# One kernel, its load list regrouped: four more token tiles turned by DMA, and five loads given out by ScalarE

## The chip, the cores and the metric

The kernel runs on one core of one Trainium2 chip. The metric is the device time of one execution in microseconds (us), the median over the runs. Everything below on times comes from three runs of the kernel before and from one more execution that was profiled.

The engines are called PE (TensorE, matrix products), ACT (ScalarE), DVE (VectorE), POOL (GpSimd) and SP (SyncE, which here does nothing but give out DMAs). "PEld" is the loading of PE's stationary operand, which overlaps its products.

## The reference

The output is `x + A(xn) + B(xn)`, with `xn = layernorm(x)` over 512 features of 2048 tokens, all in bf16. A is an attention over a sliding window, B a gated block that mixes tokens:

```
def A(xn):                                  # 32 heads of 16
    q, k, v = split(xn @ wqkv)
    logits[s, w] = q[s] . k[s - 2*w] / 4    # w = 0..7, masked where s - 2*w < 0
    return (softmax(logits) @ v[s - 2*w]) @ wo

def B(xn):                                  # w_in 512 x 1376, w_sp 2048 x 2048
    z = gelu(xn @ w_in)
    z1, z2 = z[:, :688], layernorm(z[:, 688:])
    return (z1 * (w_sp @ z2 + b_sp)) @ w_out
```

## The kernel before, in words

The 2048 tokens are 16 tiles of 128. Every engine has a list of named steps, written out by hand at the end of the kernel (`pe`, `act`, `dve`, `pool`, `sp`), and does them in that order; `needs` says which steps of other engines each step waits for. The names:

- `x0` to `x12`: loads of tokens (x0 to x5 one tile each, x6 two, x8 and x12 four each).
- `b`, `ag`, `gr`, `n` with a tile's number: the statistics of a tile (DVE, line 169), their aggregate (DVE, 172), the root (POOL, 175 and 176) and the normalised tile (DVE, 179).
- PE needs the normalised tile turned (features on partitions, in `xnT`). There are two ways. For tiles below `NPE`, `T` are four transposes of 128x128 on PE into a bank `aux` (line 212), and `Tc` is ACT's copy from there (line 215). For the others, `t` is one DMA transpose of the whole tile, given out by SP (line 195).
- `z` and `y`: the two halves of `xn @ w_in` (line 230), eight products of 128x344 each; `h` and `yg` are ACT's gelu of them (lines 248 and 312). They, and the products of q, k, v, go through a ring of three PSUM buffers `mm`: a product waits until ACT has emptied the buffer of the third one before it.
- `k`, `q`, `v` (line 323): eight products each, over all tokens, so that they wait for all 16 turned tiles; `kc`, `qc`, `vc` are ACT's copies. `kh0`: two small DMAs on SP that complete the first quarter of k (lines 341 and 342); `kh1` to `kh3` are the same on POOL.
- `m`, `f`, `p` (lines 357, 362, 369): the logits, products on DVE and sums by DMAs of POOL. Then softmax (X, u, C) and `a`, the weighted sum of v (lines 421, 425, 434), all on DVE. `a0.11` and `a1.11` are its last steps for either half of the tokens.
- `W0` to `W7` (line 448): `w_sp`, eight pieces of 1 MB, brought in by DMA transposes of SP into three buffers. W2 waits for `HW` on DVE (line 445), which stands behind the last logits; W3 and on wait for the mix that used their buffer.
- `M0` to `M15` (line 464): the mix `w_sp @ z2`, 32 products of 128x344 each; Mj uses piece W(j/2). `G` is ACT's copy (478), `g` the gate on DVE (480), `U` turns the gated tile by one or two DMA transposes of SP (470, 472, 473).
- `LO0` to `LO3` (line 485) load `wo` and `LO4` (488, 490; three DMAs) `w_out`; `R0`, `R1` (497) load x again. `gf`, `re`, `ao` (508, 513, 520) are the last products; `E`, `F`, `S` bring the sums out.
- `wz0`, `wz1`: weights of z2; `wy`: weights of z1; `wk`, `wq`, `wv`.

SP gives out in this order: `x0 x1 wz0 x2 wz1 x3 x4 x5 x6 x8 wy x12 wk wq wv`, then `t8` to `t15`, `W0 kh0 W1 vh W2 W3 LO0 LO1 U0 W4 U1 LO2 LO3 U2 W5 U3 U4 LO4 U5 W6 U6 U7 W7` and so on. PE does `z0 .. z7 y0 z8 y1 z9 .. z14`, then k and q (with z15 between), v, `y2 .. y15`, M0 to M15 and the last products.

One thing comes not from the lists but from how the program is built: DMAs of SP and ACT get one of eight completion counters in turn, and a DMA waits until the one before it on its counter has landed. With all of them on SP that is the DMA eight places ahead.

Of the kernel before, what the change touches and what calls it, by code (L numbers as in the profile page):

```python
# [26 lines left out]
FH = 688  # L27
# [15 lines left out]
def kernel(  # L43
# [47 lines left out]
    w_q, w_k, w_v = [wts[:, n * C * D:(n + 1) * C * D].rearrange("p (k f) -> p k f", k=C) for n in range(3)]  # L91
    w_z = [wts[:, C * (3 * D + n * FH):C * (3 * D + (n + 1) * FH)].rearrange("p (k f) -> p k f", k=C) for n in (1, 0)]
# [14 lines left out]
    z2 = z2_r[:].rearrange("p (i f) -> p i f", i=NT)  # L107
# [4 lines left out]
    xs = z1_r[:, 0:NT * D].rearrange("p (i d) -> p i d", i=NT)  # L112
# [30 lines left out]
    wq_d = A_wqkv.rearrange("(k p) f -> p k f", p=P)  # L143
    wi_d = B_w_in.rearrange("(k p) f -> p k f", p=P)
# [4 lines left out]
    def op_(name, after, f):  # L149
        assert name not in do, name  # L150
        do[name], needs[name] = f, list(after)

    def tok(i):
        return f"Tc{i}" if i < NPE else f"t{i}"

    NPE = 8
    ALLX = [tok(i) for i in range(NT)]
    ALLN = [f"n{i}" for i in range(NT)]


    def load_x(i, n):
        SP.dma_start(xs[:, i:i + n, :], x2[i * P:(i + n) * P, :].rearrange("(i p) d -> p i d", p=P))  # L162
# [15 lines left out]
    def norm(eng, i):  # L178
        eng.tensor_scalar(xn[i % 8], xs[:, i, :], mv[:, i, 0:1], rstd[:, i:i + 1], ALU.subtract, ALU.mult)  # L179
# [5 lines left out]
    for i in range(NT):  # L185
# [6 lines left out]
        else:  # L192
            op_(f"n{i}", [f"gr{i}"] + ([tok(i - 8)] if i >= 8 else []), lambda i=i: norm(V, i))
        if i >= NPE:
            op_(f"t{i}", [f"n{i}"], lambda i=i: SP.dma_start_transpose(xnT[:, :, i * P:(i + 1) * P], xn[i % 8]))
# [41 lines left out]
    for hh in range(2):  # L237
        op_(f"wz{hh}", [], lambda hh=hh: SP.dma_start(
            w_z[1][:, :, hh * FHALF:(hh + 1) * FHALF], wi_d[:, :, FH + hh * FHALF:FH + (hh + 1) * FHALF]))
    op_("wk", [], lambda: SP.dma_start(w_k, wq_d[:, :, D:2 * D]))  # L240
    op_("wq", [], lambda: SP.dma_start(w_q, wq_d[:, :, 0:D]))
    op_("wv", [], lambda: SP.dma_start(w_v, wq_d[:, :, 2 * D:3 * D]))
    op_("wy", [], lambda: SP.dma_start(w_z[0], wi_d[:, :, 0:FH]))
    op_("b16", [], lambda: G.dma_start(b16[:], B_b_sp.rearrange("(j p) -> j p", p=P)))

    def z2_gelu(i, t):
# [125 lines left out]
    for c, th in BUF:  # L372
        n = f"{c}{th}"
# [131 lines left out]
    def gated_full(i, start, stop, c=slice(0, D)):  # L505
        th, t0 = i // 8, (i % 8) * P
        for m in range(MF):
            PE.matmul(po[i][:, c], uT[th][:, m, t0:t0 + P], wout[:, m, c], start=(start and m == 0), stop=(stop and m == MF - 1))  # L508

    def gated_rest(tiles, start, stop):  # L510
        for i in tiles:
            r, t0 = 64 * (i // 2 % 2), (i % 8) * P
            PE.matmul(po[i], uT[i // 8][r:r + FREST, MF, t0:t0 + P], wout[r:r + FREST, MF, :],  # L513
                      start=start, stop=stop, tile_position=(r, 0))
# [6 lines left out]
                          start=(start and d == 0), stop=(stop and d == DH - 1), tile_position=(32 * g, 0))  # L521

    U = [[f"U{j}" for j in range(8 * th, 8 * th + 8)] for th in range(2)]
    EVM = [f"G{j}" for j in range(NT)] + ["Bc", "Tc4"]
    for n in (0, 1):
        op_(f"gf{n}", LO + U[0] + EVM, lambda n=n: [gated_full(i, True, False) for i in groups[n]])
        op_(f"re{n}", [f"gf{n}"], lambda n=n: gated_rest(groups[n], False, False))
# [27 lines left out]
    for n, c in enumerate(halves):  # L555
        i = groups[3][3]
# [1 line left out]
        op_(f"Sl{n}", [f"Fl{n}"], lambda n=n, c=c: (SP, A)[n].dma_start(out2[i * P:(i + 1) * P, c], o_of(i)[:, c]))  # L558
# [39 lines left out]
    dve += """zt0 zt1 zt2 zt3 zt4 zt5 zn0 zn1 zn2 zn3 zt6 zt7 zn4 zn5 zn6 zn7
# [62 lines left out]
```

## Time and profile before

| | |
|---|---|
| three runs | 205.86, 209.40 and 208.57 us; median 208.57 |
| profiled execution | 206.27 us, of which 204.5 are the span from the first to the last instruction |
| granted clock of PE in the profiled execution | 0.999 |
| PE, PEld, DVE, ACT, POOL busy | 95%, 59%, 86%, 44%, 21% of the span |
| moved by DMA | 33.63 MB, mean 164 GB/s |

The profile has a page of summaries and views that can be asked for one stretch: the timeline (start, duration, engine, line, operation, and in brackets the idle time ahead of it with what ended it), the chain of waits (the work that ended last, followed back), and tables of busy time by stretch. In all of them times are from the start of the span. SPq is SP giving out a DMA: its duration is the giving out alone, and the landing comes later. PE's clock is full throughout, so a difference in PE's work is one of work and of waits.

### The profile page before, as it was taken

How to read it: one execution, taken by the hardware profiler on the slowest of the kernel's cores; microseconds unless marked ns; L12 is line 12 of the kernel's file. 1: busy time of each engine (PE TensorE's matmuls, PEld its weight loads, DVE VectorE, ACT ScalarE, POOL GpSimd, SP SyncE). 2: the span in 40 equal slices, each digit the busy share in tenths (PEclk: the TensorE clock that was granted, in tenths of full speed). 3: DMA queues.
4: the chain of work that ended last, by engine and by line, in shares of the span. 5: the costliest groups of instructions: out<-in, count | busy, mean ns of one | idle time of the engine just before them, and what ended most of it. 6: DMA issues, size and time to landing. Idle time of an engine off the chain costs nothing.

```text
span 204.5 us, 4534 instructions
## 1 busy us (share of the span) xinstructions
PE 194.8 (95%) x1935; PEld 121.1 (59%) x1935; DVE 175.3 (86%) x202; ACT 89.9 (44%) x130; POOL 43.2 (21%) x72
## 2 busy tenths in 40 slices
PE   7899999999999999999999999999696999999991
PEld 2476666666666666666666666666464654444441
DVE  5899894897899999959999999999996699995314
ACT  2497797795569996654453311111111110052000
POOL 5577122059995033110000000000000000000000
PEclk9999999999999999999999999999999999999999
DMA  5999474919999999992699997979789499006023
GB/s 164 355 379 178 103 151 89 205 13 185 196 184 182 200 192 152 172 185 44 133 207 253 141 220 163 251 78 247 179 86 226 111 262 275 0 3 202 23 86 103
DMA packets 68388, 33.63 MB, mean 164 GB/s; under 512 B 56064, under 2 KB 66192, under 8 KB 68240
## 3 DMA queue, kind: packets, MB, share of 16 engines
q1 hardware_dynamic: 65696, 24.79, 56.3%
q0 software_dynamic: 2528, 8.48, 22.8%
q8 instruction: 15, 0.25, 0.5%
q10 hardware_dynamic: 144, 0.07, 0.1%
q14 instruction: 5, 0.04, 0.1%
HBM read 10.03 MB, written 2.10 MB: 59 GB/s over the span
## 4 chain that ended last, share of the span: by engine, by line
PE 81%; DMA 11%; DVE 5%; SPq 1%; issue 0%; DVEq 0%
PE mm L464 31%; PE mm L323 20%; PE mm L230 13%; DMA wsp<-in_B_w_sp_dram 7%; PE mm L520 7%; PE mm L508 6%; DVE stats L169 2%; DMA xnT<-z 2%; DMA z<-in_A_x_dram 2%; PE aux L508 2%; PE mm L513 1%; DVE z L179 1%; SPq L162 1%; DVE z L552 1%; DVE mv L172 1%
## 5 line engine op out<-in xcount | busy, mean ns | idle before, releaser
L464 PE MATMUL mm<-z,wsp 128*128 128x344 bf16 x512 | 75.2, 309 | 3.3 <-DMA wsp<-in_B_w_sp_dram 3.3
L464 PEld LDWEIGHTS <-wsp 128*128 128x128 bf16 x512 | 49.9, 98 | 28.4 <-DMA wsp<-in_B_w_sp_dram 4.0
L323 PE MATMUL mm<-xnT,wts 128*32 128x512 bf16 x768 | 41.9, 380 | 0.0
L230 PE MATMUL mm<-wts,xnT 128*128 128x344 bf16 x256 | 39.2, 309 | 0.6 <-ACT xnT L215 0.5
L323 PEld LDWEIGHTS <-wts 128*32 128x32 bf16 x768 | 28.4, 139 | 13.2 <-issue 0.6
L421 DVE TENSOR_TENSOR prod<-vp,a_sb 128x4096 bf16<-128x4096 bf16 x16 | 36.1, 2284 | 0.0
L478 ACT ACTIVATE qk<-mm,b_col 128x688 bf16<-128x688 f32 x16 | 13.3, 832 | 50.0 <-PE mm L464 47.8
L230 PEld LDWEIGHTS <-xnT 128*128 128x128 bf16 x256 | 24.3, 98 | 13.3 <-ACT xnT L215 0.9
L357 DVE TENSOR_TENSOR prod<-qk 128x4096 bf16<-128x4096 bf16 x12 | 26.9, 2288 | 2.1 <-DMA qk<-qk 1.9
L425 DVE TENSOR_TENSOR prod<-prod,prod 128x8192 bf16<-128x8192 bf16 x6 | 26.5, 4418 | 0.0
L336 ACT CAST qk<-mm 128x1024 bf16<-128x1024 f32 x16 | 16.2, 1012 | 7.8 <-PE mm L323 7.8
L312 ACT ACTIVATE z<-mm 128x688 bf16<-128x688 f32 x16 | 11.8, 748 | 5.6 <-PE mm L230 5.2
L520 PE MATMUL mm<-wts,xnT 32*128 32x512 bf16 x192 | 14.2, 374 | 0.0
L508 PE MATMUL mm<-wts,qk 128*128 128x512 bf16 x60 | 13.8, 379 | 0.0
L508 PEld LDWEIGHTS <-qk 128*128 128x128 bf16 x85 | 8.2, 98 | 9.4 <-issue 0.8
L362 POOL DMA_DIRECT2D prod<-prod x12 | 10.7, 1178 | 12.5 <-DVE prod L357 12.5
L248 ACT ACTIVATE z<-mm 128x688 bf16<-128x688 f32 x16 | 11.9, 745 | 2.2 <-PE mm L230 2.1
L169 DVE BATCH_NORM_STATS2 stats<-z 128x6 f32<-128x512 bf16 x16 | 10.7, 672 | 1.9 <-DMA z<-in_A_x_dram 1.9
L552 DVE TENSOR_TENSOR z<-mm,wsp 128x512 bf16<-128x512 f32 x6 | 3.9, 684 | 9.9 <-PE mm L520 5.6
L520 PEld LDWEIGHTS <-xnT 32*128 32x128 bf16 x256 | 6.4, 93 | 7.6 <-issue 0.8
L480 DVE TENSOR_TENSOR z<-qk,z 128x688 bf16<-128x688 bf16 x16 | 8.0, 510 | 3.3 <-ACT qk L478 3.3
L546 ACT CAST z<-mm 128x512 bf16<-128x512 f32 x6 | 3.2, 598 | 13.7 <-PE mm L520 12.3
(81 smaller groups left out, 170.7 us busy)
## 6 DMA issues: line engine op xcount, KB each, us to landing
prod<-prod POOLq DMA_DIRECT2D x12, 512.0 KB, 8.7
wts<-in_A_wo_dram SPq DMA_DIRECT2D x4, 512.0 KB, 6.6
wsp<-in_A_x_dram SPq DMA_DIRECT2D x2, 1024.0 KB, 5.8
out_dram<-z SPq DMA_DIRECT2D x15, 128.0 KB, 1.8
wts<-in_A_wqkv_dram SPq DMA_DIRECT2D x3, 512.0 KB, 9.3
z<-in_A_x_dram SPq DMA_DIRECT2D x2, 512.0 KB, 7.3
wsp<-z POOLq DMA_DIRECT2D x2, 512.0 KB, 8.3
wsp<-wts POOLq DMA_DIRECT2D x2, 512.0 KB, 8.3
```

The lines of the kernel that those rows point to most:

```text
L169: V.bn_stats(stats[:, i, :], xs[:, i, :])
L230: PE.matmul(t[:, hh, 0:FHALF], xnT[:, kc, i * P:(i + 1) * P], w_z[part][:, kc, hh * FHALF:(hh + 1) * FHALF], start=(kc == 0), stop=(kc == ...
L248: A.activation(z2[:, i, :].rearrange("p (a b) -> p a b", a=2), t[:, :, 0:FHALF], ACT.Gelu_apprx_tanh, **total)
L323: PE.matmul(t[32 * g:32 * g + 32, dd, :], w, r, start=(kc == 0), stop=(kc == C - 1), tile_position=(0, 32 * g))
L336: op_(f"{a}c{p}", [f"{a}{p}"], lambda: A.copy(home(a, p), t[:].rearrange("p d (t s) -> p d t s", t=2)))
L357: V.tensor_tensor(pr, q, k, ALU.mult)
L421: return lambda: V.tensor_tensor(dst, vp[:, :, th, off:off + GS], a_sb[:, th, W - 1 - w].unsqueeze(1).broadcast_to([P, DH, GS]), ALU.mult)
L425: return lambda: V.tensor_tensor(dst, dst, x, ALU.add)
L464: PE.matmul(t[:, hh, 0:FHALF], w[:, k, (j % 2) * P:(j % 2 + 1) * P], z2[:, k, hh * FHALF:(hh + 1) * FHALF], start=(k == 0), stop=(k == NT ...
L478: lambda: A.activation(gs[j % 3].rearrange("p (a b) -> p a b", a=2), t[:, :, 0:FHALF], ACT.Identity, bias=b_col[:, j:j + 1]))
L508: PE.matmul(po[i][:, c], uT[th][:, m, t0:t0 + P], wout[:, m, c], start=(start and m == 0), stop=(stop and m == MF - 1))
L520: PE.matmul(po[groups[n][g]], op[32 * g:32 * g + 32, th, d, s * P:(s + 1) * P], wo_r[32 * g:32 * g + 32, d, :], start=(start and d == 0), ...
```

## The change

Five things are edited together:

- `NPE` goes from 8 to 4: tiles 4 to 7 are turned by DMAs of SP (`t4` to `t7`) instead of by PE and ACT.
- `x12`, `wy`, `wk`, `wq`, `wv` are given out by ACT, at places inside its list, instead of by SP.
- SP's list: `x2` stands ahead of `wz0`; `t4` follows `x8` directly; `LO2 LO3` go from between U1 and U2 to behind W5, `LO4` from ahead of U5 to behind W6.
- PE's list: `B` (one small transpose of b_sp) and `y0` stand earlier, and `y2` stands between z11 and z12 instead of behind v7. ACT's list follows this.
- DVE's list: `n2` stands ahead of `b3`.

```diff
-    NPE = 8
+    NPE = 4
...
-        SP.dma_start(xs[:, i:i + n, :], ...)
+        (A if i == 12 else SP).dma_start(xs[:, i:i + n, :], ...)
...
-    op_("wk", [], lambda: SP.dma_start(w_k, wq_d[:, :, D:2 * D]))
+    op_("wk", [], lambda: A.dma_start(w_k, wq_d[:, :, D:2 * D]))
...
-    EVM = [f"G{j}" for j in range(NT)] + ["Bc", "Tc4"]
+    EVM = [f"G{j}" for j in range(NT)] + ["Bc", "Tc3"]
...
-    pe = """wu T0a T0 z0a z0A T1 z0B T2 z1 T3 z2 T4 z3 T5 z4 T6 z5 T7 B z6 z7 y0 z8 y1 z9 z10 z11 z12 z13 z14
+    pe = """wu T0a T0 z0a z0A T1 z0B T2 z1 T3 z2 B z3 z4 z5 z6 y0 z7 z8 y1 z9 z10 z11 y2 z12 z13 z14
...
-        v0 v1 v2 v3 v4 v5 v6 v7 y2 y3 y4 y5 y6 y7 y8 y9 y10 y11 y12 y13 y14 y15
+        v0 v1 v2 v3 v4 v5 v6 v7 y3 y4 y5 y6 y7 y8 y9 y10 y11 y12 y13 y14 y15
...
-    act = """GL Tc0a Tc0 Tc1 Tc2 h0 Tc3 h1 Tc4 h2 Tc5 h3 Tc6 h4 Tc7 Bc h5 h6 h7 yg0 h8 yg1 h9 sq8 h10 h11 sq9 h12 h13 h14 sq10
+    act = """GL Tc0a Tc0 Tc1 x12 Tc2 h0 wy Tc3 h1 Bc h2 wk h3 h4 wq h5 h6 yg0 wv h7 h8 yg1 h9 sq8 h10 h11 sq9 yg2 h12 h13 h14 sq10
...
-    dve = """b0 ag0 b1 ag1 n0a n0 b2 ag2 n1 b3 ag3 n2 b4 ag4 n3 b5 ag5 n4 b6 ag6 b7 n5""".split()
+    dve = """b0 ag0 b1 ag1 n0a n0 b2 ag2 n1 n2 b3 ag3 b4 ag4 n3 b5 ag5 n4 b6 ag6 b7 n5""".split()
...
-    sp = """x0 x1 wz0 x2 wz1 x3 x4 x5 x6 x8 wy x12 wk wq wv t8 t9 t10 t11 t12 t13 t14 t15 W0 kh0 W1 vh
-        W2 W3 LO0 LO1 U0 W4 U1 LO2 LO3 U2 W5 U3 U4 LO4 U5 W6 U6 U7 W7 U8 U9 U10 R0 U11 U12 U13 R1 U14 U15""".split()
+    sp = """x0 x1 x2 wz0 wz1 x3 x4 x5 x6 x8 t4 t5 t6 t7 t8 t9 t10 t11 t12 t13 t14 t15 W0 kh0 W1 vh
+        W2 W3 LO0 LO1 U0 W4 U1 U2 W5 LO2 LO3 U3 U4 U5 W6 LO4 U6 U7 W7 U8 U9 U10 R0 U11 U12 U13 R1 U14 U15""".split()
```

`wq`, `wv` and `wy` are moved to ACT in the same way as `wk`. In the program that this builds, the completion counters of the five loads on ACT come round so that x12 waits for x2, wy for wz1, wk for x8, wq for t5 and wv for t10.

More of the change, by code (lines that the diff above doesn't have):

```diff
@@ L161, in load_x @@
     def load_x(i, n):
-        SP.dma_start(xs[:, i:i + n, :], x2[i * P:(i + n) * P, :].rearrange("(i p) d -> p i d", p=P))
+        (A if i == 12 else SP).dma_start(xs[:, i:i + n, :], x2[i * P:(i + n) * P, :].rearrange("(i p) d -> p i d", p=P))
     for i, n in ((0, 1), (1, 1), (2, 1), (3, 1), (4, 1), (5, 1), (6, 2), (8, 4), (12, 4)):
@@ L239 @@
             w_z[1][:, :, hh * FHALF:(hh + 1) * FHALF], wi_d[:, :, FH + hh * FHALF:FH + (hh + 1) * FHALF]))
-    op_("wk", [], lambda: SP.dma_start(w_k, wq_d[:, :, D:2 * D]))
-    op_("wq", [], lambda: SP.dma_start(w_q, wq_d[:, :, 0:D]))
-    op_("wv", [], lambda: SP.dma_start(w_v, wq_d[:, :, 2 * D:3 * D]))
-    op_("wy", [], lambda: SP.dma_start(w_z[0], wi_d[:, :, 0:FH]))
+    op_("wk", [], lambda: A.dma_start(w_k, wq_d[:, :, D:2 * D]))
+    op_("wq", [], lambda: A.dma_start(w_q, wq_d[:, :, 0:D]))
+    op_("wv", [], lambda: A.dma_start(w_v, wq_d[:, :, 2 * D:3 * D]))
+    op_("wy", [], lambda: A.dma_start(w_z[0], wi_d[:, :, 0:FH]))
     op_("b16", [], lambda: G.dma_start(b16[:], B_b_sp.rearrange("(j p) -> j p", p=P)))
@@ L587 @@
     op_("EL", ["yg15"], lambda: A.preload_act_table_set("natural_log_exp_and_others"))
-    act = """GL Tc0a Tc0 Tc1 Tc2 h0 Tc3 h1 Tc4 h2 Tc5 h3 Tc6 h4 Tc7 Bc h5 h6 h7 yg0 h8 yg1 h9 sq8 h10 h11 sq9 h12 h13 h14 sq10
+    act = """GL Tc0a Tc0 Tc1 x12 Tc2 h0 wy Tc3 h1 Bc h2 wk h3 h4 wq h5 h6 yg0 wv h7 h8 yg1 h9 sq8 h10 h11 sq9 yg2 h12 h13 h14 sq10
         kc0 sq11 kc1 qc0 sq12 qc1 h15 kc2 sq13 kc3 sq14 qc2 sq15 qc3 kc4 kc5 qc4 qc5 kc6 kc7 qc6 qc7
         vc0 zn8 vc1 zn9 vc2 zn10 vc3 zn11 vc4 zn12 vc5 zn13 vc6 zn14 vc7 zn15
-        yg2 yg3 yg4 yg5 yg6 yg7 yg8 yg9 yg10 yg11 yg12 yg13 yg14 yg15 EL
+        yg3 yg4 yg5 yg6 yg7 yg8 yg9 yg10 yg11 yg12 yg13 yg14 yg15 EL
         G0 e0 G1 i0 e1 G2 i1 G3 G4 G5 G6 G7 G8 G9 G10 G11 G12 G13 G14 G15""".split()
     act += [f"E{i}" for n in (0, 1) for i in groups[n]]
-    dve = """b0 ag0 b1 ag1 n0a n0 b2 ag2 n1 b3 ag3 n2 b4 ag4 n3 b5 ag5 n4 b6 ag6 b7 n5""".split()
+    dve = """b0 ag0 b1 ag1 n0a n0 b2 ag2 n1 n2 b3 ag3 b4 ag4 n3 b5 ag5 n4 b6 ag6 b7 n5""".split()
     for i in range(6, NT):
```

## The prediction

> **What bounds the kernel now.** I read the page first, then the chain of waits in order of time.
>
> ```profile
> span 204.5 us, 4534 instructions
> PE 194.8 (95%) x1935; PEld 121.1 (59%) x1935; DVE 175.3 (86%) x202; ACT 89.9 (44%) x130; POOL 43.2 (21%) x72
> ...
> L464 PE MATMUL mm<-z,wsp 128*128 128x344 bf16 x512 | 75.2, 309 | 3.3 <-DMA wsp<-in_B_w_sp_dram 3.3
> ```
>
> PE is busy in 95% of the span, and the dearest group of its products, the mix, has 3.3 us of idle time ahead of it, all of it waiting for pieces of `w_sp`. The chain shows where (start, duration, what):
>
> ```profile
> 3.15 3.93 DMA z<-in_A_x_dram
> ...
> 15.25 4.24 DMA xnT<-z
> ...
> 19.54 9.51 PE mm L230 x64
> 29.04 7.07 PE mm L323 x128
> ...
> 139.02 7.13 DMA wsp<-in_B_w_sp_dram
> ...
> 149.71 7.55 DMA wsp<-in_B_w_sp_dram
> ...
> 157.31 9.51 PE mm L464 x64
> 166.81 5.40 PE mm L508 x25
> ...
> 188.83 3.77 PE mm L520 x65
> ```
>
> So: loads and statistics to 15 us, then t8, then PE without a break from 19.5 to 139 (z8 on, k, q, v, y, ten mixes), then W6 and W7, each landing late, and from 166.8 the last products. The end follows the end of M15 at 166.81 by 37.7 us of span. An edit changes the time only if it moves that 166.81, and three things can: when PE gets through the head, how late W6 and W7 land, and DVE.
>
> **The head: what goes.** The timeline of the head, and the view of the line that turns tiles by DMA:
>
> ```profile
> 7.10 0.69 DVE L169 BATCH_NORM_STATS2 stats<-z 128x6 f32<-128x512 bf16 x1 [0.25 <-DMA z<-in_A_x_dram]
> ...
> 10.17 0.39 DVE L179 TENSOR_SCALAR z<-z,mv,rstd 128x512 bf16<-128x512 bf16 x1
> ...
> 11.16 0.39 PE L212 MATMUL aux<-ident,z 128*128 128x128 bf16 x4
> ...
> 11.38 1.33 PE L230 MATMUL mm<-wts,xnT 128*128 128x344 bf16 x8
> ...
> 11.58 0.59 ACT L215 COPY xnT<-aux 128x512 bf16<-128x512 bf16 x1 [0.16 <-PE aux L212]
> 11.88 0.39 DVE L179 TENSOR_SCALAR z<-z,mv,rstd 128x512 bf16<-128x512 bf16 x1
> 12.06 0.75 ACT L248 ACTIVATE z<-mm 128x688 bf16<-128x688 f32 x1
> ...
> 12.77 1.33 PE L230 MATMUL mm<-wts,xnT 128*128 128x344 bf16 x8
> ...
> 19.53 9.16 PEld L230 LDWEIGHTS <-xnT 128*128 128x128 bf16 x64 [0.46 <-DMA xnT<-z]
> ```
>
> ```profile
> L195 SPq DMA_TRANSPOSE xnT<-z x8: 1216/1217/1631, 15.3 to 24.9; - x8
> ...
> DMA to landing us min/median/max: 2.3/2.4/4.2
> ```
>
> ```profile
> 4.00:17.00 13.00, 12.06 (x93) 7.41 (x92) 12.07 (x35) 8.64 (x16) 8.97 (x24) 1.00 1.07 359
> 17.00:19.50 2.50, 2.43 (x17) 1.40 (x15) 2.50 (x9) 1.58 (x4) 1.91 (x6) 1.00 1.15 96
> ```
>
> With a transpose on PE between them z3 and z4 start 1.39 us apart (11.38, 12.77); alone a part takes 9.51 / 8 = 1.19 (eight parts from 19.54). The four transposes so cost PE 4 x 0.20 = 0.8 us, not 4 x 0.39, since most of each ran in the shadow of products. Add the wait for t8 (0.46 in the last row): at most 1.3 us can be won in the head. ACT gets rid of four copies, 4 x 0.59, and takes five DMAs.
>
> **The head: what comes.** z4 now needs t4, and t4 needs n4. n2 (0.39 like the other norms) moves ahead of b3 and waits there for POOL's root, so b3 starts near 7.5 instead of 7.10, and n2's absence later gives back a part. I take n4 and n5 0.3 us later (bounds 0 and 0.4, one norm): they end at 10.56 + 0.3 = 10.86 and 12.27 + 0.3 = 12.57. The landing of a turned tile took 2.3 to 4.2 us; the 4.2 was t8, given out at 15.25 while DMA still moved 359 GB/s of loads at a share of 1.07 (the first stretch, to 17 us), the 2.3 and 2.4 were later ones. In the changed kernel x12, wy and wk are in flight beside t4 to t6, but on another queue, not ahead on the same one: 2.8, nearer the median. So z4 starts at 10.86 + 2.8 = 13.66, where z3 is done near 12.7 as now: PE stands about 1 us. z5 starts at 12.57 + 2.8 = 15.37, again after a stand. Behind that SP gives out one tile per 1.22 us, PE needs 1.19, and y0, y1, y2 fill, so PE follows: ten parts z5 to z14 and three y, 13 x 1.19 = 15.5, and k0 starts at 30.87.
>
> One wait is new: wv on ACT waits for t10 (same counter), and h7, h8, yg1 queue behind it. t10 is given out at 12.57 + 5 x 1.22 = 18.67 and lands at 21.47; the giving out of wv costs ACT between 0.37 and 2.83 us:
>
> ```profile
> 7.43 2.83 SPq L241 DMA_DIRECT2D wts<-in_A_wqkv_dram  x1
> ...
> 201.81 0.37 ACTq L558 DMA_DIRECT2D out_dram<-z  x1
> ```
>
> The first is wq on SP, given out while the loads kept DMA full, the second the only DMA that ACT gave out before. At 21 us the loads are through: 0.6, nearer the second. h7 ends at 21.47 + 0.6 + 0.75 = 22.8; z9, which needs its buffer, could have started at 15.37 + 6 x 1.19 = 22.5. That is 0.3 us more: k0 at 31.17, **2.1 us later** than 29.04 (with 2.3 for landing 1.3, with 4.2 throughout 3.5). wk (waits for x8) and wq (for t5) meet waits that are over by then. y2 is in this already, 1.19 us that v7 no longer has behind it, so the mix starts 2.1 - 1.2 = 0.9 us later. So the 1.3 us are not won: z4 and z5 wait for the first two tiles, and SP's 1.22 a tile keeps PE from catching up.
>
> **From k to the mix.** k0 sets kh0, kh0 the first logits, these HW, and HW the pieces from W2 on:
>
> ```profile
> 33.75 0.76 SPq L341 DMA_DIRECT2D qk<-qk  x1
> ...
> 36.51 8.90 DVE L357 TENSOR_TENSOR prod<-qk 128x4096 bf16<-128x4096 bf16 x4 [1.91 <-DMA qk<-qk]
> ```
>
> ```profile
> 98.02 9.27 SPq L448 DMA_TRANSPOSE wsp<-in_B_w_sp_dram  x2
> ...
> 109.84 9.74 SPq L448 DMA_TRANSPOSE wsp<-in_B_w_sp_dram  x1
> ...
> 124.69 6.46 SPq L448 DMA_TRANSPOSE wsp<-in_B_w_sp_dram  x1
> 132.52 2.11 SPq L473 DMA_TRANSPOSE qk<-z  x1
> ...
> 136.01 0.58 SPq L488 DMA_DIRECT2D wts<-in_B_w_out_dram  x1
> 136.64 0.98 SPq L490 DMA_DIRECT2D wts<-in_B_w_out_dram  x2
> ...
> 139.02 5.08 SPq L448 DMA_TRANSPOSE wsp<-in_B_w_sp_dram  x1
> ...
> 149.71 5.46 SPq L448 DMA_TRANSPOSE wsp<-in_B_w_sp_dram  x1
> ```
>
> DVE waited 1.91 us for kh0 at 36.51, so all of its logits move by 2.1, W2 to 100.1. From there to W7 SP's list has no gap: W7 at 149.71 is the sum of what SP gives out, and the same items stand ahead of it in the changed list. They only cost less where they are less blocked. W5 took 6.46 us behind LO2 and LO3, W6 only 5.08, W2 and W3 together 9.27: 1.4 to 1.8 saved, 1.6 taken. U3's second DMA took 2.11 behind W5 against 1.22: 0 to 0.9, 0.9 taken. Against it, LO2 and LO3 may block W6 as they did W5, though four DMAs of U now lie between, 4 x 1.22 = 4.9 us: 0 to 1.4, 0 taken. Sum 2.5 (bounds 0 and 2.7).
>
> W6 also has LO4's three DMAs behind it, 1.65: it starts at 139.02 + 2.1 - 2.5 - 1.65 = 137.0 and lands 7.13 later, 144.1. PE, which began to wait for W6 at 146.20 - 1.69 = 144.5 (the row below), is ready for M12 at 144.5 + 0.9 = 145.4: **W6's wait goes**, worth 1.7. W7 starts at 149.71 + 2.1 - 2.5 = 149.3 and lands at 156.9; PE is ready at 145.4 + 9.5 = 154.9 and stands 2.0 us. So W7 alone sets M15's end: 156.9 + 9.5 = 166.4 against 166.81, **0.4 us earlier**. Between 1.3 - 2.7 = -1.4 and 3.5 - 0 = +3.5.
>
> Behind it nothing else becomes late:
>
> ```profile
> 146.20 9.51 PE L464 MATMUL mm<-z,wsp 128*128 128x344 bf16 x64 [1.69 <-DMA wsp<-in_B_w_sp_dram]
> ...
> 163.05 0.52 DVE L480 TENSOR_TENSOR z<-qk,z 128x688 bf16<-128x688 bf16 x1 [1.59 <-ACT qk L478]
> ...
> 181.83 2.29 DVE L434 TENSOR_TENSOR xnT<-prod 128x4096 bf16<-128x4096 bf16 x1
> ```
>
> a1.11 ended at 184.12 and `ao2` began at 188.83: 4.7 us. DVE comes 2.1 later, and its waits for late mixes, of which 1.59 is the second, don't grow. LO4 in its new place is given out by 137.0 + 5.1 + 1.65 = 143.8 and is wanted at 166. The earlier B and R0, R1 at their old places cost nothing.
>
> **The sum.** 206.27 (204.5 and 1.8 around it) - 0.4 = 205.9. The three runs lie at 205.86, 208.57 and 209.40, so the profiled one is near the lowest; from the median the same sum gives 208.2. I put the time between: **207.0 us**.
>
> **Rivals.**
>
> *The tiles turned by DMA come slowly (slower).* If each transpose beside ACT's loads takes SP the 2.11 us that U3's took behind W5, in place of 1.22, t15 is given out at 12.57 + 10 x 2.11 = 33.67, lands at 36.2, and k0, which needs all tiles, starts 7.2 us late. Less the 2.5: +4.7, 211.0 (213 from the median). It decides from about 2.05 us a tile. For it: with loads in flight one of the eight took 1.63, and t8 landed after 4.2. Against it: those loads were on the same queue, and the median is 1.22. [...] Chance 0.2.
>
> *Both waits for `w_sp` go (faster).* With landings of 2.3 the mix starts 0.1 late, and if W7 lands by 154.1 the end comes 3.3 - 0.1 = 3.2 earlier: 203.1. SP would have to gain 4.2 us rather than 2.5. For it: LO4 no longer stands right ahead of W6, and every piece that starts less blocked frees SP sooner for the next. Against it: W7 waits for nothing but SP's list, and that list is no shorter. Chance 0.17. [...]
>
> *LO2 and LO3 block W6 instead of W5 (the move of SP's list gives nothing).* Then the 2.1 stays: 208.4. Chance 0.15.
>
> **How the numbers follow.** Forecast 0.48, by itself 204.9 to 209.8 (206.27 less 1.4, and more by 3.5). A difference of 2% is 4.2 us; less than about that a measurement of this kernel can't tell from none, its own runs lying 1.7% apart. Faster by more: most of the second rival against the median, and the low end of the forecast, 0.16. Slower by more: the first rival and some of the case of slow landings, 0.24. Within: 0.60. Range: from the second rival's 203.1, with a little left out, 203.6, to the first's, 211.4.
>
> **What would show it.** In the profile after: z4 idle 0.5 to 2.5 us waiting for `xnT` at 12 to 14 us; SP's DMA transposes of `xnT` x12 at 1.22; a gap on ACT near 20 us ahead of h7; line 323 starting at 30.4 to 32.5; HW near 100; line 448 at 137 with PE idle ahead of line 464 once, for 2 us, not twice. If line 323 starts by 29.5 the head is wrong; if W5's issue still takes 6 us, the gain on SP is; if both waits are gone, the second rival holds.

## The result and the profile after

The changed kernel takes **215.56 us** (median of four runs, 215.24 to 215.80), the kernel before 208.61 beside it (205.86 to 209.40): a ratio of 1.038, with a 95% interval of 1.030 to 1.046. It is slower; the forecast was 207.0 in a range that ended at 211.4. The profiled execution took 215.72 us. (In all ratios below, runs more than 1.5% above the fastest of their kernel are left out, so that a ratio can differ a little from that of two medians.)

The page of the changed kernel, in the parts that were shown of before:

```profile
span 213.9 us, 4502 instructions
...
PE 196.9 (92%) x1916; PEld 121.3 (57%) x1919; DVE 175.5 (82%) x202; ACT 87.8 (41%) x126; POOL 44.8 (21%) x72
...
PEclk9995999999999999999999999999999799999999
...
L464 PE MATMUL mm<-z,wsp 128*128 128x344 bf16 x512 | 76.8, 313 | 4.5 <-DMA wsp<-in_B_w_sp_dram 4.5
...
L230 PE MATMUL mm<-wts,xnT 128*128 128x344 bf16 x256 | 40.4, 318 | 5.9 <-DMA xnT<-z 5.5
```

Two things are new. Line 230 has 5.5 us of idle time that ended with a turned tile, and the clock granted to PE, which was full all through before, falls in the fourth and the 32nd of the 40 slices. The chain of waits says when (start, duration, what):

```profile
10.97 7.28 DMA xnT<-z
18.30 18.25 PE mm L230 x112
36.55 7.07 PE mm L323 x128
...
157.01 7.77 DMA wsp<-in_B_w_sp_dram
164.83 11.18 PE mm L464 x64
```

The first row is t4. It was given out at 10.97, the forecast's own time to 0.1 us, and landed 7.28 us later, where 2.8 were forecast; z4 starts at 18.30 instead of 13.66, and k0 (line 323) at 36.55, 7.5 us later than before. The last two rows are W7 and, behind it, M14 and M15, which take 11.18 us instead of 9.51.

**The head.** The line that turns tiles, and the busy times by stretch (us busy and number of instructions of PE, PEld, DVE, ACT, POOL; granted clock, share of DMA time, GB/s):

```profile
L195 SPq DMA_TRANSPOSE xnT<-z x12: 1216/1217/1582, 11.0 to 26.4; - x12
...
DMA to landing us min/median/max: 2.5/4.7/7.3
```

```profile
9.00:13.00 4.00, 3.23 (x23) 1.72 (x21) 3.74 (x12) 2.56 (x6) 2.85 (x8) 1.00 1.12 337
13.00:16.00 3.00, 0.00 (x0) 0.00 (x0) 3.00 (x10) 0.62 (x1) 2.30 (x7) 0.84 0.93 78
16.00:19.00 3.00, 0.70 (x3) 0.43 (x4) 3.00 (x10) 0.00 (x0) 2.27 (x7) 0.50 1.20 274
19.00:22.00 3.00, 3.00 (x13) 1.56 (x11) 2.29 (x8) 0.74 (x1) 2.22 (x5) 0.52 0.81 112
```

SP gave out its twelve tiles at 1.22 us each, as forecast. What is slow is the landing: median 4.7 us, at most 7.3, against 2.4 and 4.2 before. Beside t4 the last load given out is wk, 0.6 us behind it; here is its line:

```profile
L240 ACTq DMA_DIRECT2D wts<-in_A_wqkv_dram x1: 422/422/422, 11.6 to 11.6; - x1
...
DMA to landing us min/median/max: 6.3/6.3/6.3
```

wk is down at 11.6 + 6.3 = 17.9 and t4 at 18.25. In the second stretch of the table PE does nothing at all, and DMA, at a share of 0.93, moves 78 GB/s. To the end of the last stretch PE has half its clock (0.50 and 0.52): z4 to z14 and y0 to y2, 14 parts, would take 14 x 9.51 / 8 = 16.6 us at full clock and took 18.25, so the clock costs 1.6. (A part is eight products, as in the prediction.)

**From k to the mix.** SP's pieces of `w_sp`, to be held against 98.02, 109.84, 124.69, 139.02 and 149.71 before:

```profile
108.05 9.33 SPq L448 DMA_TRANSPOSE wsp<-in_B_w_sp_dram  x2
119.92 7.46 SPq L448 DMA_TRANSPOSE wsp<-in_B_w_sp_dram  x1
...
132.09 4.55 SPq L448 DMA_TRANSPOSE wsp<-in_B_w_sp_dram  x1
...
144.45 5.31 SPq L448 DMA_TRANSPOSE wsp<-in_B_w_sp_dram  x1
...
157.01 4.33 SPq L448 DMA_TRANSPOSE wsp<-in_B_w_sp_dram  x1
```

W2 comes 10.03 us later, W7 only 7.30: SP's list saves 2.73 us between them, and W5 is given out in 4.55 us instead of 6.46. But k0 was only 7.51 late, and W2 is 10.03. The 2.5 us between lie at one instruction, a copy of one element by POOL (step `HF`, line 444), which makes POOL wait for W1 and stands ahead of `kh1` in its list. Before (first fence) and after:

```profile
36.51 8.90 DVE L357 TENSOR_TENSOR prod<-qk 128x4096 bf16<-128x4096 bf16 x4 [1.91 <-DMA qk<-qk]
43.08 0.18 POOL L444 COPY hold<-wsp 1x1 bf16<-1x1 bf16 x1 [10.08 <-DMA wsp<-in_B_w_sp_dram]
43.33 0.90 POOL L341 DMA_DIRECT2D qk<-qk  x1
```

```profile
44.01 8.90 DVE L357 TENSOR_TENSOR prod<-qk 128x4096 bf16<-128x4096 bf16 x4 [9.05 <-DMA qk<-qk]
50.69 2.26 POOL L444 COPY hold<-wsp 1x1 bf16<-1x1 bf16 x1 [17.33 <-DMA wsp<-in_B_w_sp_dram]
52.90 0.90 POOL L341 DMA_DIRECT2D qk<-qk  x1
```

The same copy takes 0.18 us before and 2.26 after. After, it ends at 50.69 + 2.26 = 52.95, where DVE's four multiplications end (44.01 + 8.90 = 52.91). Before, it fell on the seam between the third and the fourth (36.51 + 3 x 8.90 / 4 = 43.19). So HW's delay is 7.51 (k0) + 0.10 (W1 lands 7.94 instead of 7.84 us after it is given out) + 2.08 (the copy) + 0.34 (what is left over, in the rest of the logits) = 10.03.

**The sum.** 10.03 - 2.73 + 0.22 (W7 lands in 7.77 instead of 7.55) = 7.52: M14 starts at 164.83, not 157.31. The clock adds 1.67 to M14 and M15, and the rest of the span 0.2. That is 9.4, the difference of the spans (213.9 - 204.5).

### The profile page after: what moved, and what is told of

Read it like the earlier page. It is cut to its first block, busy times and chain, and to the rows that moved or that the text cites. A ratio compares the mean times of both kernels' runs of the same rounds, so it can differ in the third digit from the quotient of the medians.

```text
span 213.9 us, 4502 instructions
## 1 busy us (share of the span) xinstructions
PE 196.9 (92%) x1916; PEld 121.3 (57%) x1919; DVE 175.5 (82%) x202; ACT 87.8 (41%) x126; POOL 44.8 (21%) x72
## 3 DMA queue, kind: packets, MB, share of 16 engines
HBM read 10.03 MB, written 2.10 MB: 57 GB/s over the span
## 4 chain that ended last, share of the span: by engine, by line
PE 51%; DVE 31%; DMA 12%; issue 2%; POOL 1%; SPq 1%; ACT 0%; DVEq 0%
PE mm L323 20%; PE mm L230 11%; DVE prod L421 8%; PE mm L520 6%; DVE prod L425 6%; PE mm L508 6%; PE mm L464 5%; DMA prod<-prod 4%; DMA wsp<-in_B_w_sp_dram 4%; DMA xnT<-z 3%; DVE prod L357 3%; DVE z L480 2%; PE aux L508 2%; DVE stats L169 1%; DVE a_sb L370 1%
## 5 line engine op out<-in xcount | busy, mean ns | idle before, releaser
L464 PE MATMUL mm<-z,wsp 128*128 128x344 bf16 x512 | 76.8, 313 | 4.5 <-DMA wsp<-in_B_w_sp_dram 4.5
L464 PEld LDWEIGHTS <-wsp 128*128 128x128 bf16 x512 | 50.6, 99 | 30.6 <-DMA wsp<-in_B_w_sp_dram 3.6
L230 PE MATMUL mm<-wts,xnT 128*128 128x344 bf16 x256 | 40.4, 318 | 5.9 <-DMA xnT<-z 5.5
L230 PEld LDWEIGHTS <-xnT 128*128 128x128 bf16 x256 | 25.1, 100 | 19.9 <-DMA xnT<-z 5.8
L176 POOL TENSOR_TENSOR rstd<-rstd,mhalf 128x1 f32<-128x1 f32 x16 | 9.0, 562 | 1.3
```

Source lines behind the costliest of these rows:

```text
L230: PE.matmul(t[:, hh, 0:FHALF], xnT[:, kc, i * P:(i + 1) * P], w_z[part][:, kc, hh * FHALF:(hh + 1) * FHALF], start=(kc == 0), stop=(kc == ...
L464: PE.matmul(t[:, hh, 0:FHALF], w[:, k, (j % 2) * P:(j % 2 + 1) * P], z2[:, k, hh * FHALF:(hh + 1) * FHALF], start=(k == 0), stop=(k == NT ...
```

## The experiments

The theory after the result had three parts: (1) a turned tile doesn't land while loads are in flight beside it, whoever gave them out; (2) the copy of line 444 is long wherever it meets a multiplication of DVE, in the kernel before too; (3) PE's idle times are paid twice, since the clock is lowered behind a long one. Rivals: ACT's queue is what delays the tiles; the tiles need no loads to be slow; the lateness is only SP's.

### The loads given out by SP again

```diff
-        (A if i == 12 else SP).dma_start(xs[:, i:i + n, :], ...)
+        SP.dma_start(xs[:, i:i + n, :], ...)
...
-    sp = """x0 x1 x2 wz0 wz1 x3 x4 x5 x6 x8 t4 t5
+    sp = """x0 x1 x2 wz0 wz1 x3 x4 x5 x6 x8 wy x12 wk wq wv t4 t5
```

(wk, wq, wv and wy the same; the rest of the change stays.)

> The changed kernel with x12, wy, wk, wq and wv given out by SP again, ahead of t4; nothing else undone. Theory (two queues: a tile turned by SP lands only when the loads that ACT gave out around it have landed, and while both are in flight DMA moves little): with everything on one queue DMA stays above 330 GB/s until about 17 us, without the hole of 70 GB/s at 13 to 16 us, t4 waits behind the loads and lands at 18 to 19.5, and the tiles behind it follow every 1.2 to 1.4 us, each within 4 us of being given out, t15 before 29. PE still stands 5 to 6.5 us ahead of z4; time 212 to 217. Rival (transposes of DMA are slow whenever loads are near, whatever the queue): the hole stays, t4 lands after 20, time over 217.

Measured: 217.87 us (217.44 to 218.33), 1.041 times before (1.036 to 1.046). t4 is given out at 10.98 and lands 7.71 us later, at 18.69, and k0 starts at 37.90. The time is 0.9 us over the theory's 217, but of the rival's signs neither came: there is no hole, and t4 lands ahead of 20. With the loads ahead on the same queue DMA moves 371 to 375 GB/s to 16 us, with no stretch at 78, and the tile comes no sooner. So neither ACT's queue nor that poor stretch is the cause: t4 waits in both cases until the loads are down (wv, the last of them here, at 9.5 + 8.7 = 18.2). The tile took 7.28 us with the loads on another queue and 7.71 with them on its own.

### The loads given out late

```diff
-    act = """... Tc2 h0 wy Tc3 h1 Bc h2 wk h3 h4 wq h5 h6 yg0 wv h7 h8 yg1 h9 ...
+    act = """... Tc2 h0 Tc3 h1 Bc h2 h3 h4 h5 h6 h7 wk h8 wq h9 sq8 h10 h11 sq9 wv h12 ...
```

(wy behind kc1; y0 to y2 back behind v7 on PE.)

> The changed kernel with wk, wq, wv and wy given out by ACT only from behind h7 on, so that beside t4 to t8 only x12 is in flight, and y0, y1, y2 done behind v7. Theory (two queues): t4 lands 2.3 to 3.5 us after it is given out, at 13.3 to 14.5; PE stands about 1 us ahead of z4 and its granted clock stays at 1; line 323 starts at 28 to 31; time 204 to 209. Rival (the early transposes are slow by themselves): t4 still takes over 6 us and PE stands over 5 us; time over 212.

Measured: 209.84 us (208.09 to 211.53), 1.001 times before (0.997 to 1.005). PE's waits in the head, and the stretch after wk was given out at 19.07:

```profile
13.47 1.34 PE L230 MATMUL mm<-wts,xnT 128*128 128x344 bf16 x8 [0.62 <-DMA xnT<-z]
15.08 5.22 PE L230 MATMUL mm<-wts,xnT 128*128 128x344 bf16 x32 [0.27 <-DMA xnT<-z]
22.30 1.58 PE L230 MATMUL mm<-wts,xnT 128*128 128x344 bf16 x8 [2.00 <-DMA xnT<-z]
24.69 8.64 PE L230 MATMUL mm<-wts,xnT 128*128 128x344 bf16 x40 [0.81 <-DMA xnT<-z]
```

```profile
19.00:21.00 2.00, 1.30 (x9) 0.66 (x8) 2.00 (x7) 1.41 (x3) 1.62 (x4) 1.00 1.16 69
```

With no weights in flight t4 lands in 2.4 us and z4 starts at 13.47, near the forecast's 13.66. Then the loads come, and it is t9 and t10 that land after 4.3 and 5.4 us, though wk was given out *after* t9 (17.9). So here a load delayed a tile whether it was given out ahead of it or shortly behind. It doesn't always hold the tile to its own end: t9 is down at 22.2, wk only at 19.1 + 5.1 = 24.2. The theory's k0 at 28 to 31 and its full clock were missed: behind the waits for t9 and t10 the granted clock falls (0.56 from 23 to 25 us, 0.50 from 25 to 29), and k0 starts at 24.69 + 8.64 = 33.33. By the medians, on two chips, this kernel beats the changed one by 5.7 us, which is the price of the loads' place together with that of y0 to y2, which were moved with them.

### wy early, the others late

```diff
-    act = """... h0 wy Tc3 h1 Bc h2 wk h3 h4 wq h5 h6 yg0 wv h7 h8 yg1 h9 sq8 h10 h11 sq9 yg2 h12 ...
+    act = """... h0 wy Tc3 h1 Bc h2 h3 h4 h5 h6 yg0 h7 wk h8 yg1 wq h9 sq8 h10 h11 sq9 yg2 wv h12 ...
```

> The changed kernel with wk, wq and wv given out by ScalarE behind h7 and later; x12 and wy (w_in's first half, given out at 8.2 us) stay where the change has them. Theory: a turned tile lands only when what DMA has in flight beside it is down, whichever was given out first; wy alone (1.4 MB by its shape of 512 by 1376 in 16 bits) is down near 13.5 to 14.5, so t4 lands at 14.5 to 16, PE stands 1.5 to 3 us, the granted clock stays at 1 there, k0 comes at 32.5 to 34.5, and the time is 211 to 213. Rival one: only a load given out behind the tile (wk, 0.6 us behind t4) holds it: then t4 lands at 13.4 to 13.8 as with all loads late, k0 at 31 to 32, time 209 to 210. Rival two: the first turned tile is slow by itself: t4 lands at 17 or later.

Measured: 213.40 us (210.50 to 213.89), 1.012 times before (1.002 to 1.021). The chain has:

```profile
10.93 5.11 DMA xnT<-z
16.09 18.19 PE mm L230 x112
```

wy (688 KB; the 1.4 MB above counted both halves of `w_in`) is down at 8.56 + 6.9 = 15.5, t4 at 16.04. PE stands 3.3 us, a little over the theory's 3, and the clock falls even so (0.74 from 16 to 19 us), so k0 comes at 34.28. In all three kernels t4 lands just behind the last load that was given out ahead of it or 0.6 us behind it: 18.25 behind wk at 17.9 in the changed one, 17.2 behind wk at 17.0 in the one with the copy changed (below), 16.04 behind wy at 15.5 here. Where wk came later behind t4, it did not hold it: in one more profile of this head (the head alone, below) wk was given out 1.6 us behind t4 and was down at 18.5, and t4 landed at 15.95, behind wy at 15.3. Both rivals fall, the second with t4 at 16.04 where it had 17 or later.

### Tiles 4 to 7 turned by PE again

```diff
-    NPE = 4
+    NPE = 8
...
-    pe = """... T3 z2 B z3 z4 z5 z6 y0 z7 ...
+    pe = """... T3 z2 T4 z3 T5 z4 T6 z5 T7 B z6 y0 z7 ...
```

(ACT's copies back in its list, t4 to t7 out of SP's; loads still on ACT, SP's new order.)

> The changed kernel with tiles 4 to 7 turned by PE and ACT again; the loads stay on ACT, SP's list keeps its new order behind t15. Theory (the loss needs both: loads of ACT in flight, and PE waiting for a tile that is turned beside them): t8, given out near 15.5, meets what is left of wk and lands late by some us, after 18.5, but PE has work until 19, so it stands under 2.5 us; line 323 starts by 31; time 204 to 210. Rival (giving the loads out on ACT is the whole loss, by itself): PE stands over 4 us in the head, time over 212.

Measured: 209.35 us (208.08 to 211.56), before 208.94 on that chip; no interval was formed. PE waits 0.7 us for a turned tile in place of 5.5 and keeps its clock (1.0 in the profiled execution; a product of line 230 takes 309 ns, as before, and 318 in the changed kernel). t8, now the first of SP's, lands after 4.7 us, and k0 starts at 32.03, a little behind the theory's 31 and still 3.0 later than before. So of the head's 7.5 us some 4.5 hang on the four tiles.

### PE kept busy while it waits for t4

```diff
+    op_("wm", ["Tc3", "wu"], lambda: [PE.matmul(aux[1][:], warm[:, 0:P], warm, start=True, stop=True) for _ in range(18)])
...
-    pe = """... T3 z2 B z3 z4 z5
+    pe = """... T3 z2 B z3 wm z4 z5
```

> The changed kernel, with 18 more products of zeros on TensorE between z3 and z4 (they write a bank that is rewritten later), so that TensorE is busy for about 5 us while t4 comes. Theory: of the 7.5 us by which k0 comes later, some 1.6 are products at the half clock after 5.5 us of idle time; then the granted clock stays at 1 in the head, z4 starts near 18.3 as before and k0 at 34.7 to 35.2 rather than 36.55; the time comes down by 1 to 2 us unless the copy of line 444 meets another gap of VectorE (2.2 us steps). Rival: the clock is no term of its own (k0 waits for the last turned tile, given out by SP): k0 stays at 36 or later.

Measured: 215.15 us (214.20 to 216.71), 1.025 times before (1.021 to 1.030). The clock stays at 1.00 in the head and k0 starts at 35.08, the theory's time, but in part by luck: z4 started at 17.01, not 18.3, since t4 landed after 6.0 us. The clock's part can still be read: from z4 to k0 are 18.07 us, of which 1.41 are a wait of PE for ACT, and the other 16.66 are the 14 parts at full clock. That wait came because ACT stood 3.33 us at the place of wq until a turned tile had landed:

```profile
22.46 0.74 ACT L248 ACTIVATE z<-mm 128x688 bf16<-128x688 f32 x1 [3.33 <-DMA xnT<-z]
```

W2 comes at 107.58, only 0.5 us sooner than in the changed kernel, so in the profiled execution little of the gain reaches the end. The ratios (1.025 against 1.038) leave room for more, and their intervals touch. The clock is a term of the head, but not the one that decides.

### The copy made a DMA, in the kernel before and in the changed one

```diff
-    op_("HF", ["W1"], lambda: G.tensor_copy(hold[0:1, 0:1], wsp_r[1][0:1, 0:1]))
+    op_("HF", ["W1"], lambda: G.dma_start(hold[0:1, 0:2], wsp_r[1][0:1, 0:2]))
```

In the kernel before:

> The kernel before, with GpSimd's one-element copy of a piece of w_sp (line 444, HF) made a small DMA on GpSimd instead. Theory: the copy waits for VectorE's long multiplication of line 357 whenever it comes after the gap between two of them, and so every launch but the rare one where W1 lands just ahead of a gap (as in the profiled run of before, 0.18 us for the copy) pays up to 2.3 us on the way to HW. Then without the copy HW stands at 97.9 to 98.8 in every launch, the median comes down from 208.6 to 206.0 to 207.3 and the runs lie within 1 us. Rival: the copy's length doesn't matter, since the waits for W6 and W7 take it up, or the 2 us between launches of before have another cause: median 208 to 209, still spread over 3 us.

Measured: 208.45 us (206.78 to 209.52), 0.996 times before (0.992 to 1.000), as the rival had it. In the changed kernel:

> The changed kernel, with the one-element copy of line 444 made a small DMA on GpSimd. Theory: of the 10.0 us by which HW comes later, 2.3 to 2.5 are the copy standing behind VectorE's multiplication; HW then comes at 105.4 to 106 rather than 107.95, W7 at 154.5 to 155, and PE's wait for W7 shrinks from 3.2 us to about 1, so that the clock stays up for M14: 211.5 to 213.5. Rival: the copy was short in this place by itself or another thing holds HW: 215 to 216.

Measured: 212.43 us (210.84 to 214.41), 1.011 times before (1.007 to 1.016). W2 comes at 106.30 instead of 108.05, but 1.1 of that are a k0 that came earlier (35.47, with t4 landing after 6.3 us); PE's wait for W7 stays at 3.35 us, and M14 and M15 at 11.18. So the time lies in the theory's range, but not by the theory's way: the profiled execution, the longest of the four, shows no shorter wait, and why the others are shorter is not shown. Counted from k0, W2 comes after 69.9 and 70.8 us in these two kernels (100.10 - 30.16 and 106.30 - 35.47); with the copy it is 71.5 in the changed kernel, 71.1 and 71.4 in two profiles of before with SP's new order (below), and 69.0 in the profiled execution of before alone. Over all profiles here it is 71.1 to 72.5 us in the twelve whose copy took 1.5 us or more and 69.9 to 70.8 in the four with the DMA. So the DMA, which takes POOL 0.61 us, is worth about 0.7 to 1.5 us where the theory had 2.3, and the launches of before don't close up: their spread has other causes as well, which stay open. One is seen: in the profile of the first of these runs PE's first products were slow (z0's half of four took 1.33 us, 0.76 in two others), though the granted clock reads 1.00 there, and k0 came at 30.16 rather than 29.04. What slowed them is not shown.

### SP's new order alone

```diff
-        W2 W3 LO0 LO1 U0 W4 U1 LO2 LO3 U2 W5 U3 U4 LO4 U5 W6 U6
+        W2 W3 LO0 LO1 U0 W4 U1 U2 W5 LO2 LO3 U3 U4 U5 W6 LO4 U6
```

The kernel before with this alone, then with this and the copy made a DMA:

> The kernel before with one edit: LO2 and LO3 behind W5 and LO4 behind W6 in SP's list. In the changed kernel W5 took 4.55 us to give out instead of 6.46 and W6 did not make PE wait. Theory (SP's list behind the mix gains 2.5 to 2.9 us, hidden in the changed kernel by the head): PE's wait for W6 goes, W7 starts 2 to 3 us earlier, the idle time ahead of line 464 falls from 3.3 to under 1 us; time 1.0 to 1.6% under before. Rival (W7 was late by 7.3 us only because all was late, and the order gives nothing): within 0.4% of before.

> As the one before, and SP's list from W4 on in the order of the change (LO2 and LO3 behind W5, LO4 behind W6), nothing else of the change. Theory: SP gives out W7 2.5 to 2.7 us sooner, W6 in time and W7 at most 1 us late, so that 2 to 3.3 us go on top of the first gain: 203.0 to 204.5, faster than both kernels. Rival: the new order only moves the wait: 206 to 207, as the copy's edit alone.

Measured: 208.16 us (203.03 to 211.20; four runs, no interval was formed) for the first, where before has 208.94 on that chip, and 207.81 (205.28 to 208.85) for the second, which is 0.987 times before (0.981 to 0.992). That is the lowest ratio here, a gain of 1.3%, with an interval that leaves out 1 but not the 0.989 of the order alone on another chip (below), and less than the theory said. The first theory's signs did not come: in its profile W7 is given out at 150.46, not sooner than before, and PE waits 0.44 us for W6 and 2.89 for W7, behind which M14 and M15 take 11.18; the copy took 1.73 us there. The pieces W5, W6, W7 in the kernel with the copy alone changed and, second, with SP's order too:

```profile
126.61 6.74 SPq L448 DMA_TRANSPOSE wsp<-in_B_w_sp_dram  x1
141.22 4.89 SPq L448 DMA_TRANSPOSE wsp<-in_B_w_sp_dram  x1
151.72 5.61 SPq L448 DMA_TRANSPOSE wsp<-in_B_w_sp_dram  x1
```

```profile
124.85 4.17 SPq L448 DMA_TRANSPOSE wsp<-in_B_w_sp_dram  x1
137.93 4.40 SPq L448 DMA_TRANSPOSE wsp<-in_B_w_sp_dram  x1
149.59 5.05 SPq L448 DMA_TRANSPOSE wsp<-in_B_w_sp_dram  x1
```

W2 stood at 100.10 and 99.67, so the order alone makes W6 2.9 and W7 1.7 us sooner.

### The loads late and the copy a DMA, in the changed kernel

(Both edits from above.)

> The changed kernel with wk, wq, wv and wy given out by ScalarE from behind h7 on (y0 to y2 back behind v7), and the copy of line 444 made a small DMA on GpSimd. Theory: with the loads out of the way of t4 to t8 the head costs 1 to 3 us, the copy's edit takes some 1 us off HW, and SP's order 2.5 us off W7: 207 to 209 where before runs at 208.4 to 209.7, a ratio of 0.985 to 1.0. Rival: t9 to t11 behind the late loads cost as much as t4 did: 210 or more.

Measured: 209.62 us (208.19 to 210.82), 1.000 times before (0.997 to 1.004): above the theory's time, at the end of its ratio. The late loads still cost the head waits of 1.80 and 1.59 us and some clock (0.83 from 22 to 26 us, 0.74 from 26 to 30), and k0 comes at 32.49.

### What the order is worth beside the new head

The changed kernel with SP's list from W2 on as it was before (the diff above, reversed):

> The changed kernel with SP's list from W2 on as it was before (LO2 and LO3 ahead of W5, LO4 ahead of W6). Theory: the new order of that list gains 2.5 to 2.7 us at W7, so without it W5's issue is back at 6 to 6.7 us, W7 comes at 159 to 160 and the time is 217.5 to 219. Rival: with the mix 8.5 us late all round the order is worth nothing: 215 to 216.3.

Measured: 216.88 us (215.00 to 217.25), 1.033 times before (1.026 to 1.041). The mechanism is there (W5 is given out in 6.55 us, W7 at 159.75, 2.7 later), but the time lies between the theory's and the rival's, and the ratio is no worse than the changed kernel's on another chip. PE now waits ahead of M10, M12 and M14, for 1.82, 1.84 and 1.69 us, and M14 and M15 take 9.51 us. So all four combinations were run on one chip (the order is SP's new order from W2 on, the head is all the rest of the change), and the changed kernel with PE kept busy ahead of M14:

```diff
+    op_("wm", ["zn15"], lambda: [PE.matmul(aux[1][:, 0:FHALF], z2[:, 0, 0:P], z2[:, 0, 0:FHALF], start=True, stop=True) for _ in range(20)])
...
-        M0 M1 M2 M3 M4 M5 M6 M7 M8 M9 M10 M11 M12 M13 M14 M15
+        M0 M1 M2 M3 M4 M5 M6 M7 M8 M9 M10 M11 M12 M13 wm M14 M15
```

> The changed kernel with 20 more products of 344 columns on TensorE between M13 and M14 (into a bank that is rewritten later; by 9.51 us for 64 products of the mix some 3.0 us in all, just under the 3.23 us that PE waited there for W7). Theory: M14 and M15 took 11.18 rather than 9.51 us because the clock was lowered while PE waited; then they take 9.51, start where W7 lands as before, and the time falls by 1.5 to 1.8 us against the unaltered changed kernel. Rival: the wait for W7 is all, or the fillers push M14 back by what they win: within 0.5 us of the unaltered one.

> The changed kernel unaltered, beside the other three on one chip: 215 to 216.5 (1.030 to 1.038 times before). It is the corner with both parts for the three others.

> The kernel before with SP's new order from W2 on alone. Theory: W7 comes 2.1 to 2.7 us sooner, but where the two or three waits of before (each under 2 us) become one of 2.5 to 3 us, the clock is lowered in some launches and gives 1.7 us back: 1 to 2 us faster than before in the median, now and then 4. Rival: all of it is seen: 2.5 us or more in the median.

> The changed kernel with the old order of SP's list from W2 on. Theory as in the run above, from the other side: W7 2.7 us later than with the new order, but three waits of under 2 us each and no lowered clock in the mix, so the end comes only 0.8 to 1.3 us later than with both parts. Rival: the whole 2.5 us are lost, or nothing.

| | median us (runs) | ratio to before |
|---|---|---|
| neither | 209.32 (207.94 to 210.29) | |
| order alone | 208.65 (205.58 to 211.74) | 0.989 (0.983 to 0.995) |
| head alone | 215.05 (211.64 to 217.55) | 1.019 (1.010 to 1.027) |
| both | 215.60 (214.44 to 217.22) | 1.032 (1.026 to 1.038) |
| both, PE busy ahead of M14 | 213.98 (212.74 to 214.58) | 1.023 (1.018 to 1.028) |

The head costs 5.7 us by the medians with the old order and 7.0 with the new. The order alone gains 0.7 by the medians, 1.1% by the ratio; beside the head it gains nothing that these runs show, less than the theory's 0.8 to 1.3, and they are too wide to say more. In the profiles SP takes 51.35 to 51.69 us from W2 to W7 with the old order (four profiles), 49.85 to 50.13 with the new order and the old head (three), 48.55 to 50.81 with the new order and the new head or a part of it (ten). What becomes of the gain is seen with both parts (PE's row, then the table of its stretch with the granted clock) and with the 20 products (the same two):

```profile
165.12 11.19 PE L464 MATMUL mm<-z,wsp 128*128 128x344 bf16 x64 [3.56 <-DMA wsp<-in_B_w_sp_dram]
```

```profile
165.00:169.00 4.00, 3.88 (x16) 2.13 (x17) 4.00 (x2) 0.00 (x0) 0.00 (x0) 0.57 0.52 116
```

```profile
161.69 3.08 PE L452 MATMUL aux<-z 128*128 128x344 bf16 x20
164.95 9.51 PE L465 MATMUL mm<-z,wsp 128*128 128x344 bf16 x64 [0.18 <-DMA wsp<-in_B_w_sp_dram]
```

```profile
165.00:169.00 4.00, 4.00 (x28) 2.70 (x29) 4.00 (x3) 0.00 (x0) 0.00 (x0) 1.00 0.48 107
```

M14 starts at the same time, but with full clock it and M15 take 9.51 us, and the kernel is 1.6 us faster by the medians, as the theory said: behind the one long wait 1.7 us were lost in clock. The head alone, which is the same kernel as the one above with three short waits and no loss, had another course in its second profile: ahead of the last three pairs PE waited once, and the clock fell behind that (M12 to M15):

```profile
157.11 20.74 PE L464 MATMUL mm<-z,wsp 128*128 128x344 bf16 x128 [2.25 <-DMA wsp<-in_B_w_sp_dram]
```

Two pairs at full clock are 2 x 9.51 = 19.02 us; here the granted clock is 6 tenths in the 30th slice of the page (156.5 to 161.8 us), and 1.7 us are lost behind a wait of 2.25. Ahead of M14 waits of 1.6 to 2.55 us were followed by 9.51 us, those of 2.77 to 3.56 by 11.18. But the clock also fell behind 2.25 us ahead of M12 here, behind 2.50 ahead of M4 in the kernel with PE busy in the head (6 tenths in the 22nd slice of its page), and behind 2.00 in the head with the loads given out late. So no one length divides the waits that cost clock from the others: 2.55 once cost nothing and 2.25 cost 1.7.

The copy, in the profile of the order alone:

```profile
36.41 8.90 DVE L357 TENSOR_TENSOR prod<-qk 128x4096 bf16<-128x4096 bf16 x4 [1.65 <-DMA qk<-qk]
43.20 2.16 POOL L444 COPY hold<-wsp 1x1 bf16<-1x1 bf16 x1 [10.03 <-DMA wsp<-in_B_w_sp_dram]
45.31 0.90 POOL L341 DMA_DIRECT2D qk<-qk  x1
```

It starts 0.12 us later than in the profiled execution of before, just misses the end of a multiplication, and takes 2.16 us, to the end of the next (45.31): W2 then comes at 100.32, though k0 is no later (28.95). Of the thirteen profiles that have the copy, it took 1.5 to 2.3 us in twelve; the one with 0.18 is the one that the forecast was made from.

## Why the prediction was wrong

**Where it failed: "but on another queue, not ahead on the same one: 2.8, nearer the median".** t4 took 7.28 us, 6.0 to 6.8 in five more profiles with the same head, and 4.8 in a sixth. The range of the row used (2.3 to 4.2) ended far below. Its 4.2 was t8, given out at 15.25, and it was no mild case of loads that were nearly through. The line of wv, the last load that SP gave out ahead of t8 in the kernel before:

```profile
L242 SPq DMA_DIRECT2D wts<-in_A_wqkv_dram x1: 1379/1379/1379, 10.3 to 10.3; - x1
...
DMA to landing us min/median/max: 8.7/8.7/8.7
```

wv was down at 10.3 + 8.7 = 19.0 and t8 at 19.49, just behind it: the profile of before already showed a tile held until a load was down, and 4.2 was short only because t8 was given out late. t4 is given out while wy and wk still have 4 and 7 us to go. That a queue of one's own gives a tile its own way was assumed, and the run with the loads moved back to SP (7.71 us) shows it false. This one step carries 4.64 us (18.30 against 13.66); PE, once it started so late, no longer had the later waits that were forecast (0.9).

**What was left out: the clock.** The forecast counted waits at their own length; what stands ahead of it says that PE's clock is full throughout, which held for the kernel before only. Behind 5.5 us without work the head lost 1.6 us more, and behind W7 1.67. Both sizes were measured, and both went when PE was kept busy in the wait (granted clock 1.00 in the head, and 1.00 from 165 to 169 us).

**"so all of its logits move by 2.1, W2 to 100.1".** That HW follows k0 rigidly holds but for the copy of line 444. Its 0.18 us in the profiled execution was luck by 0.1 us, and the forecast never looked at it: 2.1 us, on the way to every piece from W2 on. It may also be one reason why that execution was 2.3 us under the median, though without the copy the launches of before still spread over 2.7 us; the forecast took the time between the two without asking why they differ.

**What held.** SP gives out a turned tile in 1.22 us beside loads as without (the median of either kernel; at most 1.63 before and 1.58 after). So the first rival's cause did not come, and that its k0, 7.2 us late, lies near the measured 7.5 is luck. t4 was given out at 10.97 for a forecast 10.86. W6's wait goes; W7's is left, 3.2 us and not 2.0, and a new one of 1.25 us comes ahead of M4, which uses W2. Nothing behind M15 becomes late (0.2 us). The second rival, both waits gone, needed a mix that was on time; the third did not happen.

**What held in its sum alone.** The order was to save SP 2.5 us, and 2.73 were measured. W5 gave 1.91 for 1.6 and U3's second DMA 0.88 for 0.9, but W4, on which nothing was put, gave 2.28 (7.46 instead of 9.74), and U1, U4, U5 and W6 together took 2.4 back. With the old head the new order saved 1.5 to 1.8 us, so part of the match is luck. The price of wv's wait on ACT, 0.3, is unseen in the changed kernel, where ACT waits for PE anyway. "wk (waits for x8) and wq (for t5) meet waits that are over by then" did not hold where PE was earlier: there ACT stood 3.33 us at wq's place for a turned tile. And "PE without a break from 19.5 to 139" with ten mixes is where the chain leaves PE, not where PE stops: it works to 146.20 - 1.69 = 144.5, the time that the forecast itself uses for W6.

With 7.28 for the landing and 1.6 for the clock in its place, the forecast's own sum gives k0 at 36.5 and, less the 2.5, some 211.3; the copy (2.1), the second loss of clock (1.7) and 0.6 of small terms make the rest.

## What to carry to other kernels

Here a turned tile landed just behind the loads that were given out ahead of it or within 0.6 us behind it, whoever gave out either (at 18.25 behind wk at 17.9 from ACT, at 18.69 behind wv at 18.2 from SP), and a load 1.2 us behind it still cost it 2 us (4.3 instead of 2.4): before a step is handed from an engine to such a DMA, add up what is in flight at that time, and take no landing time from a quieter stretch (2.4 us there, 7.28 here). Ask of every new wait of PE whether it may lower the clock, since then it costs more than its length; here 1.6 or 1.7 us more, behind waits of about 2 us and more, and not behind every one of them. And before a profile is extrapolated, ask why its execution is faster than the median: some short instruction may have slipped between two long ones, as the copy of 0.18 us did here, which otherwise took 1.5 to 2.3.

## What the hardware showed that was not expected

- Turned tiles of 128 KB landed in 2.3 to 2.4 us with no load beside them; t4, and t9 and t10 with the loads given out late, took 4.3 to 7.7 with loads of 512 to 688 KB in flight, also where the load was given out after the tile. In some executions DMA moved only 69 to 78 GB/s for 2 to 3 us meanwhile, at a share near 1; in the changed kernel with the copy made a DMA it moved 220, and t4 still took 6.3 us. Why transposes and loads get on so badly was not tried further.
- PE's granted clock fell behind waits of about 2 us and more (1.80 and 1.59 us close together are the shortest), but not behind each of them (2.55 cost nothing once). A fall cost 1.7 us in the mix and, in the changed kernel's head, 1.6.
- A copy of one element by POOL took 1.5 to 2.3 us beside DVE's multiplications of 128x4096 from two inputs, 0.18 between two of them. In the changed kernel and in the order alone it ended with the multiplication that ran (52.95 against 52.91, 45.36 against 45.31); why it waits for that was not shown.
